# Two feeds for TensorE in a windowed-attention and gated feed-forward kernel, and the attention output taken off PSUM by ACT

## The chip, the cores and the metric

One core of one Trainium2 chip runs the kernel. The metric is the device time of one execution in microseconds. Three runs of the kernel before gave 276.29 (median), 275.74 and 276.56.

## The reference

The input is x of 2048 rows and 448 columns. The output is x plus an attention branch plus a gated feed-forward branch, both on the same normalised rows:

```python
H = 16; Dh = D // H; W = 256                      # D = 448, Dh = 28
qkv = (x @ wqkv) ...                              # q, k, v per head
scores = einsum("bhqd,bhkd->bhqk", q, k) * (Dh ** -0.5)
mask = (idx[:, None] - idx[None, :] >= 0) & (idx[:, None] - idx[None, :] < W)
p = softmax(where(mask, scores, -1e9))
A = einsum("bhqk,bhkd->bhqd", p, v) ... @ wo
B = (gelu(xn @ w_gate) * (xn @ w_up)) @ w_down    # F = 1792
out = x + A(xn) + B(xn)                           # xn = layernorm(x)
```

Each row attends to itself and the 255 rows ahead of it.

## The kernel before

The rows are worked in four blocks (`qb`) of 512 queries. A block has an attention stage and a gated stage, and the work of its neighbours is filled in between.

The attention stage (`attention`) runs over four head groups `g` of four heads each, and for each over three portions `n` of key tiles. A portion computes scores `sc` on TensorE (L373; two PSUM tiles of two banks each, tag "s"), two Exps on ACT into `p_sb` (L378), and the mask on Pool by affine selects (L384). Two portions later `finish` multiplies by the values into `ov` (L348; one bank, tag "o"). The values carry a column of ones, so `ov` also has the softmax's sums. After the third portion of a head group VectorE takes `ov` out: a transpose (L353), a copy of the sums to `l_all` (L354), a reciprocal (L356), a transpose back (L358) and a multiplication by `ov` into `oN` (L359). Both L353 and L359 read `ov` in PSUM. The last two portions of a block are finished by `rest`, which the gated stage calls ahead of its step f=2.

Between the portions `feed` issues other TensorE work, a share at a time. It holds a list of generators and takes the first one to its end before it goes to the next. For blocks 1 and 2 the list is `gen_down(qb - 1)`, the output projection of the block before (for each row tile four matmuls by `wo`, L247, and fourteen by `wd`, L251, into one bank `po`, then VectorE adds x, L256, and SP writes the rows out), and then `gen_proj(qb + 1)`: transposes `tp` of the next block's rows (L177, copied to `xnT`, L178), values `pv` (L205 casts them to `v_sb`), queries and keys `pq`, `pk` (L221, L222 cast them to `qT`, `kT`). In block 3 the second generator is `gen_up`, which makes the `up` half `ue` of the last gated stage ahead of time. All of these take their banks from tag "m", three banks. `aux` brings statistics (L144) and normalisation (L158) of the next block's rows to VectorE, one step after each portion, two calls a portion.

The gated stage (`gated`) runs over the 14 column tiles of F in steps of two: gate `gt` (tag "s") and up `u` (three of four from "m", the fourth from "o"), gelu on ACT (L318), and the product `hT` on VectorE (L320). In each step of two the last 64 rows of the depth are taken by "halves" (L187), two of which run side by side. ACT loads the tables of exp and gelu by turns (L451, L458).

The order of each engine's instructions is that in which the program issues them; tiles of one tag wait until the last reader of the bank is done. Ahead of block 0 stand the loads on SP's and ACT's queues (L89 to L114), warming matmuls `wps`, normalisation of block 0, its values, the padded copies `wqp`, `wkp`, `w3p` of the query and key weights, and the queries and keys of head group 0.

Of the kernel before, what the change touches and what calls it, by code (L numbers as in the profile page):

```python
# [24 lines left out]
class Feed:  # L25


    def __init__(self):
        self.gens = []
        self.left = 0  # L30

    def add(self, gen, ns):
        self.gens.append(gen)
        self.left += ns

    def run(self, ns):
        while ns > 0 and self.gens:
            try:
                c = next(self.gens[0])
                ns -= c  # L40
                self.left -= c
            except StopIteration:
                self.gens.pop(0)

    def share(self, parts):

        self.run(max(self.left, 0) / parts if parts > 1 else 1e12)


@with_exitstack  # L50
def kernel(
# [26 lines left out]
    wraw = blk.tile([P, 4, 2 * D], bf16, name="wraw", tag="hT", bufs=1)  # L78
# [57 lines left out]
    def warmup(n):  # L136
        for _ in range(n):
            wps = psum.tile([P, QB], f32, name="wps", tag="m", bufs=3)
# [15 lines left out]
    def norm(t):  # L154
        xn = work.tile([P, 4, P], bf16, name="xn", bufs=4)
        xf = xn[:, :, :].rearrange("p a b -> p (a b)")
        for lo, n, src in ((0, D, 0), (D, 64, 384)):
            nc.vector.tensor_scalar(out=xf[:, lo:lo + n], in0=x_sb[:, t, src:src + n], scalar1=mv_all[:, t, 0:1],  # L158
# [3 lines left out]
    def gen_prep(qb):  # L162

        for t in range(4 * qb, 4 * qb + 4):
            stat(t)
            yield
        rstd(4 * qb, 4)
        yield
        for t in range(4 * qb, 4 * qb + 4):
            norm(t)  # L170
            yield

    def transp(t, copy):
        xn = xns.pop(t)
        tp = psum.tile([P, 4, P], bf16, name="tp", tag="m", bufs=3)
# [14 lines left out]
    done = set()  # L190

    def gen_v(qb, ts):

        for t in ts:
            pvs = []
            for i in range(2):
                pv = psum.tile([P, QB], f32, name="pv", tag="m", bufs=3)
# [6 lines left out]
            for i in range(2):  # L204
                (nc.vector.tensor_copy if qb else nc.scalar.copy)(out=v_sb[:, t + i, :, 0:Dh], in_=pvs[i][:, 0:D].rearrange("p (h d) -> p h d", d=Dh))  # L205
            yield 390

    def gen_qk(qb, gs):

        ts = slice(qb * QB, (qb + 1) * QB)  # L210
        for g in gs:
            hs = slice(4 * g, 4 * g + 4)
            pq = psum.tile([P, QB], f32, name="pq", tag="m", bufs=3)
            mm3(pq[:, :], lambda c: wqp[:, c, hs, :].rearrange("p h d -> p (h d)"), lambda c: xnT[:, c, ts], True, False)
            yield 650
            pk = psum.tile([P, QB], f32, name="pk", tag="m", bufs=3)
# [7 lines left out]
            yield 1050  # L224
# [14 lines left out]
    def gen_down(qb):  # L239

        hT, oN = hTs[qb], oNs[qb]
        for tt in range(4):
            t = 4 * qb + tt
            cs = slice(tt * P, (tt + 1) * P)
            po = psum.tile([P, QB], f32, name="po", tag="m", bufs=3)
# [12 lines left out]
            yield 375  # L258

    def new_hT(qb):  # L260
        hT = blk.tile([P, NF, QB], bf16, name="hT", tag="hT", bufs=1)
        hTs[qb] = hT
# [10 lines left out]
    def gen_up(qb, fs):  # L273

        ts = slice(qb * QB, (qb + 1) * QB)
        for f in fs:
            us = [psum.tile([P, QB], f32, name="ue", tag="m", bufs=3) for _ in range(2)]
# [7 lines left out]
            yield 1050  # L285

    def gated(qb, early, then):
# [4 lines left out]
        for f in range(0, NF, 2):  # L292
            if f == 2:
                then()
# [11 lines left out]
            for _ in range(2):  # L306
                tag, n = ("m", 3) if nu % 4 < 3 else ("o", 1)
                us.append(psum.tile([P, QB], f32, name="u0", tag=tag, bufs=n))
                nu += 1
            three(gt[:, 0, :], f, True, ts, True, False)  # L310
            three(us[0][:, :], f, False, ts, True, False)
            half(gt[:, 0, :], f, True, 0, ts, False, True)
            half(us[0][:, :], f, False, 1, ts, False, True)
            half(gt[:, 1, :], f + 1, True, 0, ts, True, False)
            half(us[1][:, :], f + 1, False, 1, ts, True, False)
            three(gt[:, 1, :], f + 1, True, ts, False, True)
            three(us[1][:, :], f + 1, False, ts, False, True)
# [17 lines left out]
    def attention(qb, feed, aux, lag):  # L335
        oN = blk.tile([P, 4, QB], bf16, name="oN")
        oNs[qb] = oN
        pend = []
        o_t = {}

        def finish(g, n, pc, p_sb):
# [9 lines left out]
            if n == 2:  # L351
                l1 = work.tile([P, 16, 32], f32, name="l1", bufs=2)
                nc.vector.transpose(out=l1[:, :, :].rearrange("p a b -> p (a b)"), in_=ov[:, :])  # L353
                nc.vector.tensor_copy(out=l_all[:, 4 * qb + g, :], in_=l1[:, :, Dh])  # L354
# [241 lines left out]
```

## Time and profile before

| | us | share of the span |
|---|---|---|
| profiled execution | 276.25 | |
| its span, first to last instruction | 274.5 | |
| TensorE busy | 239.5 | 87% |
| VectorE busy | 150.1 | 55% |
| ACT busy | 133.7 | 49% |
| Pool busy | 75.7 | 28% |

Mean granted TensorE clock: 0.975. Busy times are those of the one profiled execution. A time in square brackets behind a row is how long the engine stood idle ahead of it, and what ended that. Matmuls overlap, so the starts of consecutive groups tell more than the durations of single ones. Start times count from the span's start.

### The profile page before, as it was taken

The numbers are of one execution on the slowest core, as the hardware profiler recorded it, in microseconds if no ns is written. First come the engines' busy times: TensorE is split into PE (matmuls) and PEld (weight loads), VectorE is DVE, ScalarE is ACT, GpSimd is POOL, SyncE is SP. The second block draws the span as 40 slices with busy tenths as digits, with TensorE's granted clock in tenths as the row PEclk, the third lists the DMA queues.
The fourth block names the chain that finished last, engine by engine and source line by source line (L and its number), as shares of the span: only waits on it lengthen the run. The fifth ranks groups of instructions, "written<-read, shape, count | busy, mean of one in ns | idle before, by whom it ended". The sixth has DMA issues, their size and how long they took to land.

```text
span 274.5 us, 4234 instructions
## 1 busy us (share of the span) xinstructions
PE 239.5 (87%) x1695; PEld 93.3 (34%) x1714; DVE 150.1 (55%) x294; ACT 133.7 (49%) x154; POOL 75.7 (28%) x104
## 2 busy tenths in 40 slices
PE   7867877889999969779999988797999998899992
PEld 2323322233344523223334442232334442233450
DVE  6579687423363865653363875744342167856410
ACT  4554456313386646613366583652337656765200
POOL 6222545000034553400006443510004444530000
PEclk9999999979999989999999997999999999999997
DMA  7999500000001100000000010000000010000010
GB/s 201 362 260 268 190 2 0 0 0 4 0 1 35 33 4 0 0 2 0 0 0 19 18 36 0 2 0 0 2 0 17 19 35 2 0 0 2 17 35 26
DMA packets 9025, 10.94 MB, mean 40 GB/s; under 512 B 616, under 2 KB 7976, under 8 KB 9000
## 3 DMA queue, kind: packets, MB, share of 16 engines
q1 hardware_dynamic: 8552, 10.27, 12.7%
q10 hardware_dynamic: 448, 0.34, 0.5%
q8 instruction: 15, 0.25, 0.4%
q14 instruction: 10, 0.08, 0.1%
HBM read 8.77 MB, written 1.84 MB: 39 GB/s over the span
## 4 chain that ended last, share of the span: by engine, by line
PE 67%; DVE 19%; ACT 6%; issue 2%; DMA 2%; POOL 1%; SPq 0%; ACTq 0%; DVEq 0%; POOLq 0%
PE po L251 14%; PE gt L182 14%; PE u L182 8%; PE ov L348 4%; PE gt L187 4%; PE sc L373 4%; PE po L247 4%; PE pv L182 3%; ACT p_sb L378 3%; DVE rb L358 3%; DVE oN L359 3%; DVE l L353 3%; PE ue L182 3%; PE pq L182 2%; ACT ge L318 2%
## 5 line engine op out<-in xcount | busy, mean ns | idle before, releaser
L378 ACT ACTIVATE p_sb<-sc 128x1024 bf16<-128x1024 f32 (+2 forms) x96 | 87.7, 968 | 56.3 <-PE sc L373 53.1
L384 POOL TENSOR_SCALAR_AFFINE_SELECT p_sb<-p_sb 128x512 bf16<-128x512 bf16 (+1 forms) x92 | 69.5, 778 | 162.8 <-ACT p_sb L378 162.8
L320 DVE TENSOR_TENSOR hT<-ge,u 128x512 bf16<-128x512 bf16 x42 | 27.0, 684 | 47.1 <-ACT ge L318 47.1
L318 ACT ACTIVATE ge<-gt 128x1024 bf16<-128x1024 f32 x21 | 21.5, 1024 | 53.7 <-PE gt L182 53.7
L251 PE MATMUL po<-wd,hT 128*128 128x448 bf16 x224 | 47.3, 353 | 0.0
L182 PE MATMUL gt<-xnT,wg 128*128 128x512 bf16 x164 | 45.8, 389 | 1.0 <-ACT p_sb L378 0.8
L182 PE MATMUL u<-xnT,wu 128*128 128x512 bf16 x123 | 34.6, 385 | 0.2
L251 PEld LDWEIGHTS <-hT 128*128 128x128 bf16 x224 | 20.6, 98 | 20.7 <-issue 3.2
L373 PE MATMUL sc<-qT,kT 32*128 32x128 bf16 (+2 forms) x352 | 22.2, 281 | 4.2 <-ACT p_sb L378 1.7
L348 PE MATMUL ov<-p_sb,v_sb 128*32 128x128 bf16 (+2 forms) x352 | 18.3, 286 | 8.6 <-DVE oN L359 8.2
L182 PEld LDWEIGHTS <-wu 128*128 128x128 bf16 x168 | 15.6, 99 | 20.3 <-issue 4.2
L182 PEld LDWEIGHTS <-wg 128*128 128x128 bf16 x168 | 13.8, 99 | 24.2 <-issue 12.8
L256 DVE TENSOR_TENSOR res<-po,x_sb 128x448 bf16<-128x448 f32 x16 | 9.9, 620 | 18.6 <-PE po L251 18.6
L187 PE MATMUL u<-xnT,wgu 64*128 64x512 bf16 x42 | 13.2, 382 | 5.9 <-DVE oN L359 5.9
L221 DVE CAST qT<-pq 128x512 bf16<-128x512 f32 x16 | 11.0, 686 | 13.4 <-PE pk L187 13.4
L158 DVE TENSOR_SCALAR xn<-x_sb,mv_all,rstd_all 128x448 bf16<-128x448 bf16 (+1 forms) x32 | 12.6, 441 | 8.7 <-ACT rstd_all L150 8.6
L182 PE MATMUL pv<-wv,xnT 128*128 128x448 bf16 x48 | 12.0, 379 | 4.8 <-DVE v_sb L205 4.4
L353 DVE STREAM_TRANSPOSE l<-ov 128x512 f32<-128x512 f32 x16 | 11.4, 710 | 8.1 <-PE ov L348 8.1
L187 PE MATMUL gt<-xnT,wgu 64*128 64x512 bf16 x49 | 15.3, 382 | 0.0
L247 PE MATMUL po<-wo,oN 128*128 128x448 bf16 x64 | 14.8, 353 | 0.0
L182 PE MATMUL pk<-xnT,wkp 128*128 128x512 bf16 x46 | 12.9, 379 | 2.0 <-DVE qT L221 1.9
L348 PEld LDWEIGHTS <-v_sb 128*32 128x32 bf16 x352 | 6.0, 95 | 23.5 <-issue 19.5
(66 smaller groups left out, 214.6 us busy)
## 6 DMA issues: line engine op xcount, KB each, us to landing
out_dram<-res SPq DMA_DIRECT2D x16, 112.0 KB, 1.7
wd<-in_B_w_down_dram SPq DMA_DIRECT2D x1, 1568.0 KB, 13.3
wu<-in_B_w_up_dram SPq DMA_DIRECT2D x1, 1344.0 KB
wg<-in_B_w_gate_dram SPq DMA_DIRECT2D x1, 1344.0 KB, 16.6
x_sb<-in_A_x_dram SPq DMA_DIRECT2D x1, 896.0 KB
wraw<-in_A_wqkv_dram SPq DMA_DIRECT2D x1, 672.0 KB, 7.9
x_sb<-in_A_x_dram SPq DMA_DIRECT2D x1, 448.0 KB
wo<-in_A_wo_dram SPq DMA_DIRECT2D x4, 98.0 KB
```

The lines of the kernel that those rows point to most:

```text
L158: nc.vector.tensor_scalar(out=xf[:, lo:lo + n], in0=x_sb[:, t, src:src + n], scalar1=mv_all[:, t, 0:1], scalar2=rstd_all[:, t:t + 1], op0= ...
L182: nc.tensor.matmul(ps, lhsT=lhs(c), rhs=rhs(c), start=start and c == 0, stop=stop and c == 2, skip_group_check=True)
L187: nc.tensor.matmul(ps, lhsT=lhs[p0:p0 + 64], rhs=rhs[p0:p0 + 64], start=start, stop=stop, tile_position=(p0, 0), skip_group_check=True)
L247: nc.tensor.matmul(po[:, 0:D], lhsT=oN[:, g, cs], rhs=wo[:, g, :], start=(g == 0), stop=False, skip_group_check=True)
L251: nc.tensor.matmul(po[:, 0:D], lhsT=hT[:, f, cs], rhs=wd[:, f, :], start=False, stop=(f == NF - 1), skip_group_check=True)
L318: nc.scalar.activation(out=ge[:, :, :], in_=gt[:, :, :], func=ACT.Gelu_apprx_tanh)
L320: nc.vector.tensor_tensor(out=hT[:, f + i, :], in0=ge[:, i, :], in1=us[i][:, :], op=ALU.mult)
L348: nc.tensor.matmul(ov[32 * j:32 * j + 32, q0:q0 + nq], lhsT=v_sb[:, kt, h, :], rhs=p_sb[:, j, col:col + nq], start=(n == 0 and i == 0), st ...
L353: nc.vector.transpose(out=l1[:, :, :].rearrange("p a b -> p (a b)"), in_=ov[:, :])
L373: nc.tensor.matmul(ss[j // 2][:, j % 2, col:col + nq], lhsT=kT[r, g, kt * P:(kt + 1) * P], rhs=qT[r, g, qb * QB + q0:qb * QB + q0 + nq], s ...
L378: nc.scalar.activation(out=p_sb[:, 2 * i:2 * i + 2, 0:ncol], in_=ss[i][:, :, 0:ncol], func=ACT.Exp, scale=SCALE)
L384: nc.gpsimd.affine_select(out=reg, in_=reg, pattern=mid + [[1 if diag else -1, P]], compare_op=ALU.is_ge, fill=0.0, base=0 if diag else -1 ...
```

## The change

- The output projection and the next block's projections become two feeds. `share` hands out both in portions. A generator marks the end of a closed group (one whose banks are now being evacuated) by a negative number, and `share` then takes the other feed, if that one has work left for this portion.
- PSUM: "m" has two banks, and a bank "d" is new. `gen_down` takes "o" for its first tile, then "d". Values, queries and keys of block 0 and of block 1's projections go round "m", "m", "d" (`bank`), later ones use "m". In the gated stage `u` takes by turns two "m", or "d" and "o". `hT` has two buffers.
- The attention output is copied out of `ov` by ACT (`oc`). VectorE's transposes read `oc` and are issued behind the portion's fed work (`inverse`). The multiplication into `oN` is done by Pool, behind the affine selects of the portion after (`scale_o`).
- Statistics of blocks 2 and 3 are made in the gated stages of blocks 0 and 1; `rstd` and `norm` of the next block stand ahead of the attention (`prep`). Those of block 1 are made early in block 0.
- At the start two loads change queues, two `xnT` copies go from ACT to VectorE, and the first queries and keys come ahead of the second pair of values. The gated stage's first step issues `u` ahead of `gt`.

```diff
+    def run(self, ns):
+        ran = 0
+        while ran < ns and self.gens:
             try:
                 c = next(self.gens[0])
+                self.closed = c < 0
+                c = abs(c)
+                ran += c
                 self.left -= c
...
+def share(feeds, parts):
+    want = [max(f.left, 0) / parts if parts > 1 else 1e12 for f in feeds]
+    last = None
+    while any(f.gens and w > 0 for f, w in zip(feeds, want)):
+        can = [i for i, f in enumerate(feeds) if f.gens]
+        if last in can and len(can) > 1 and feeds[last].closed and want[1 - last] > -800:
+            can.remove(last)
+        last = max(can, key=lambda i: min(want[i], feeds[i].left))
+        want[last] -= feeds[last].run(1)
...
     for p0 in (0, 64):
-        nc.scalar.dma_start(out=wv[p0:p0 + 64, 3, :], in_=A_wqkv[384:448, 2 * D:3 * D])
-    nc.sync.dma_start(out=wraw[:, 0:3, :], in_=rows(A_wqkv, 0, 3)[:, :, 0:2 * D])
+        nc.sync.dma_start(out=wv[p0:p0 + 64, 3, :], in_=A_wqkv[384:448, 2 * D:3 * D])
+    nc.scalar.dma_start(out=wraw[:, 0:3, :], in_=rows(A_wqkv, 0, 3)[:, :, 0:2 * D])
...
+    ring = [("m", "m", "d"), 0]
+    def bank(name):
+        tag = ring[0][ring[1] % len(ring[0])]
+        ring[1] += 1
+        return psum.tile([P, QB], f32, name=name, tag=tag, bufs=2 if tag == "m" else 1)
...
-    def gen_down(qb):
+    def gen_down(qb, tags="dddd"):
...
-            po = psum.tile([P, QB], f32, name="po", tag="m", bufs=3)
+            po = psum.tile([P, QB], f32, name="po", tag=tags[tt], bufs=2 if tags[tt] == "m" else 1)
...
-            for _ in range(2):
-                tag, n = ("m", 3) if nu % 4 < 3 else ("o", 1)
+            for tag, n in ((("m", 2), ("m", 2)), (("d", 1), ("o", 1)))[nu % 2]:
                 us.append(psum.tile([P, QB], f32, name="u0", tag=tag, bufs=n))
...
+        def inverse():
+            while copied:
+                g, oc = copied.pop(0)
+                l1 = work.tile([P, 16, 32], f32, name="l1", bufs=1)
+                nc.vector.transpose(out=l1[:, :, :].rearrange("p a b -> p (a b)"), in_=oc[:, :])
+                nc.vector.tensor_copy(out=l_all[:, 4 * qb + g, :], in_=l1[:, :, Dh])
+                ri = work.tile([P, 16], f32, name="ri")
+                nc.vector.reciprocal(out=ri[:, :], in_=l_all[:, 4 * qb + g, :])
+                rb = work.tile([P, 16, 32], f32, name="rb", bufs=2)
+                nc.vector.transpose(out=rb[:, :, :], in_=ri[:, :].unsqueeze(2).to_broadcast([P, 16, 32]))
+                later.append((g, oc, rb))
+
+        def scale_o():
+            while later:
+                g, oc, rb = later.pop(0)
+                nc.gpsimd.tensor_tensor(out=oN[:, g, :], in0=oc[:, :], in1=rb[:, :, :].rearrange("p a b -> p (a b)"), op=ALU.mult)
...
             if n == 2:
...
-                nc.vector.tensor_tensor(out=oN[:, g, :], in0=ov[:, :], in1=rb[:, :, :].rearrange("p a b -> p (a b)"), op=ALU.mult)
+                oc = work.tile([P, QB], f32, name="oc", bufs=2)
+                nc.scalar.copy(out=oc[:, :], in_=ov[:, :])
+                copied.append((g, oc))
...
-                for _ in range(2):
-                    next(aux, None)
-                feed.share(12 - 3 * g - n)
+                scale_o()
+                left = 12 - 3 * g - n
+                if qb and left > 10:
+                    feeds[0].share(left / 2)
+                else:
+                    share(feeds, left + 0.4 if left > 1 else 1)
+                inverse()
+                next(aux, None)
...
-    transp(2, nc.scalar.copy)
-    norm(3)
-    transp(3, nc.scalar.copy)
-    warmup(3)
+    norm(3, nc.vector)
+    transp(2, nc.vector.tensor_copy)
+    transp(3, nc.vector.tensor_copy)
+    warmup(2)
...
-    for _ in gen_v(0, (2,)):
-        pass
+    stat(4)
+    for gen in (gen_qk(0, (0,)), gen_v(0, (2,))):
+        for _ in gen:
+            pass
+    stat(5)
...
-            feed.add(gen_down(qb - 1), DOWN)
+            ring[0] = ("m",)
+            feeds = [Feed(gen_down(qb - 1, "oddd"), DOWN)]
             if qb < 3:
-                feed.add(gen_proj(qb + 1), PROJ)
-                aux = gen_prep(qb + 1)
+                feeds.append(Feed(gen_proj(qb + 1), PROJ))
+                prep(qb + 1)
...
+        hooks = {2: rest}
+        if qb < 2:
+            for i in range(4):
+                hooks[4 + 2 * i] = lambda t=4 * qb + 8 + i: stat(t)
```

## Rows read from the trace of the kernel before

**Rows 1.** Busy time by stretch: length, PE, PEld, DVE, ACT, POOL, clock, DMA.

```profile
142.03:179.40 37.37, 33.29 (x299) 13.70 (x300) 23.82 (x50) 23.28 (x26) 17.25 (x22) 0.95 0.04 14
...
206.89:242.50 35.61, 33.04 (x289) 12.60 (x292) 18.56 (x33) 22.90 (x24) 17.25 (x22) 1.00 0.04 14
```

**Rows 2.** Who waited for whom, TensorE: us in total, times, longest us.

```profile
PE ov L348 <- DVE oN L359: 8.2, 6, 1.8
PE u L187 <- DVE oN L359: 5.9, 3, 2.1
PE pv L182 <- DVE v_sb L205: 4.4, 2, 2.2
```

**Rows 3.** The chain of waits from 162 to 167 us: start, us, what.

```profile
162.30 0.73 DVE l L353
163.05 0.43 DVE l_all L354
...
164.54 0.69 DVE oN L359
...
165.81 1.28 PE pv L182 x3
```

**Rows 4.** Busy time by stretch, the columns of rows 1: four shorter stretches.

```profile
165.81:168.61 2.80, 2.79 (x22) 0.63 (x21) 1.48 (x3) 0.00 (x0) 0.69 (x1) 0.50 0.00 0
...
190.71:193.94 3.23, 3.23 (x18) 1.20 (x17) 1.27 (x2) 1.02 (x1) 0.00 (x0) 1.00 0.00 0
16.09:28.00 11.91, 9.44 (x84) 3.82 (x86) 11.13 (x27) 7.43 (x11) 4.04 (x6) 1.00 1.06 254
28.00:47.89 19.89, 14.77 (x125) 5.38 (x125) 14.89 (x27) 10.45 (x16) 9.43 (x14) 1.00 0.17 57
```

**Rows 5.** Instructions in order of time, TensorE, block 2: start, us, instruction, idle before.

```profile
140.76 0.39 PE L373 MATMUL sc<-qT,kT 32*128 32x128 bf16 x6 [0.35 <-ACT ge L318]
...
144.01 0.39 PE L373 MATMUL sc<-qT,kT 32*128 32x384 bf16 x6 [0.21 <-ACT p_sb L378]
...
176.98 0.40 PE L348 MATMUL ov<-p_sb,v_sb 128*32 128x128 bf16 x8 [1.58 <-DVE oN L359]
...
179.37 0.82 PE L182 MATMUL gt<-xnT,wg 128*128 128x512 bf16 x3
...
187.16 0.39 PE L187 MATMUL u<-xnT,wgu 64*128 64x512 bf16 x1 [1.90 <-DVE oN L359]
...
205.04 0.23 PE L373 MATMUL sc<-qT,kT 32*128 32x128 bf16 x2
```

**Rows 6.** Instructions in order of time, TensorE, start and block 0.

```profile
7.85 1.31 PE L182 MATMUL pv<-wv,xnT 128*128 128x448 bf16 x6 [0.43 <-DMA wv<-in_A_wqkv_dram]
...
30.54 0.40 PE L348 MATMUL ov<-p_sb,v_sb 128*32 128x128 bf16 x8 [1.25 <-DVE oN L359]
...
47.89 0.81 PE L182 MATMUL gt<-xnT,wg 128*128 128x512 bf16 x3 [0.76 <-ACT p_sb L378]
...
75.31 0.23 PE L373 MATMUL sc<-qT,kT 32*128 32x128 bf16 x2
```

**Rows 7.** Groups by line and shape, ACT and Pool: busy us, mean ns, idle.

```profile
L378 ACT ACTIVATE p_sb<-sc 128x512 bf16<-128x512 f32 x8 | 4.3, 594 | 8.2 <-PE sc L373 8.2
...
L149 ACT ACTIVATE lnv<-mv_all,eps_t 128x4 f32<-128x4 f32 x3 | 0.9, 298 | 0.5 <-DVE mv_all L145 0.5
...
L384 POOL TENSOR_SCALAR_AFFINE_SELECT p_sb<-p_sb 128x1024 bf16<-128x1024 bf16 x28 | 30.8, 1101 | 115.2 <-ACT p_sb L378 115.2
```

**Rows 8.** Instructions in order of time, VectorE, block 0, and one of block 2.

```profile
14.74 0.69 DVE L221 CAST qT<-pq 128x512 bf16<-128x512 f32 x1 [2.75 <-PE pk L187]
...
27.15 0.70 DVE L353 STREAM_TRANSPOSE l<-ov 128x512 f32<-128x512 f32 x1
...
30.31 0.41 DVE L178 COPY xnT<-tp 128x512 bf16<-128x512 bf16 x1
...
185.17 0.17 DVE L354 COPY l_all<-l 128x16 f32<-128x16 f32 x1
```

More of the change, by code (lines that the diff above doesn't have):

```diff
@@ L25, with __init__ @@
 class Feed:
[L28 to L34, printed above, removed]
+    def __init__(self, gen=None, ns=0):
+        self.gens = [gen] if gen else []
+        self.left = ns
+        self.closed = False
     def run(self, ns):
-        while ns > 0 and self.gens:
+        ran = 0
+        while ran < ns and self.gens:
             try:
                 c = next(self.gens[0])
-                ns -= c
+                self.closed = c < 0
+                c = abs(c)
+                ran += c
                 self.left -= c
@@ L196, in gen_v @@
             for i in range(2):
-                pv = psum.tile([P, QB], f32, name="pv", tag="m", bufs=3)
+                pv = bank("pv")
                 cs = slice((t + i) * P, (t + i + 1) * P)
@@ L204, in gen_v @@
             for i in range(2):
-                (nc.vector.tensor_copy if qb else nc.scalar.copy)(out=v_sb[:, t + i, :, 0:Dh], in_=pvs[i][:, 0:D].rearrange("p (h d) -> p h d", d=Dh))
-            yield 390
+                (nc.vector.tensor_copy if qb or (t and i) else nc.scalar.copy)(out=v_sb[:, t + i, :, 0:Dh], in_=pvs[i][:, 0:D].rearrange("p (h d) -> p h d", d=Dh))
+            yield -390
     def gen_qk(qb, gs):
@@ L276, in gen_up @@
         for f in fs:
-            us = [psum.tile([P, QB], f32, name="ue", tag="m", bufs=3) for _ in range(2)]
+            us = [psum.tile([P, QB], f32, name="ue", tag="m") for _ in range(2)]
             three(us[0][:, :], f, False, ts, True, False)
@@ L284, in gen_up, with gated @@
             nc.vector.tensor_copy(out=hTs[qb][:, f + 1, :], in_=us[1][:, :])
-            yield 1050
-    def gated(qb, early, then):
+            yield -1050
+    def gated(qb, early, hooks):
         ts = slice(qb * QB, (qb + 1) * QB)
@@ L333, in pieces, with attention @@
         return [(k - 1, 0, 256, 0), (k + 2, 256, 256, 256)], [(128, 1, False), (256, 1, True)]
-    def attention(qb, feed, aux, lag):
+    def attention(qb, feeds, aux, lag):
         oN = blk.tile([P, 4, QB], bf16, name="oN")
         oNs[qb] = oN
-        pend = []
+        pend, copied, later = [], [], []
         o_t = {}
+        def inverse():
[13 more added lines that the diff above has]
+                nc.gpsimd.tensor_tensor(out=oN[:, g, :], in0=oc[:, :], in1=rb[:, :, :].rearrange("p a b -> p (a b)"), op=ALU.mult)
         def finish(g, n, pc, p_sb):
@@ L351, in finish @@
             if n == 2:
-                l1 = work.tile([P, 16, 32], f32, name="l1", bufs=2)
-                nc.vector.transpose(out=l1[:, :, :].rearrange("p a b -> p (a b)"), in_=ov[:, :])
-                nc.vector.tensor_copy(out=l_all[:, 4 * qb + g, :], in_=l1[:, :, Dh])
-                ri = work.tile([P, 16], f32, name="ri")
-                nc.vector.reciprocal(out=ri[:, :], in_=l_all[:, 4 * qb + g, :])
-                rb = work.tile([P, 16, 32], f32, name="rb", bufs=2)
-                nc.vector.transpose(out=rb[:, :, :], in_=ri[:, :].unsqueeze(2).to_broadcast([P, 16, 32]))
-                nc.vector.tensor_tensor(out=oN[:, g, :], in0=ov[:, :], in1=rb[:, :, :].rearrange("p a b -> p (a b)"), op=ALU.mult)
+                oc = work.tile([P, QB], f32, name="oc", bufs=2)
+                nc.scalar.copy(out=oc[:, :], in_=ov[:, :])
+                copied.append((g, oc))
+        if qb:
+            feeds[0].run(1)
         for g in range(4):
             while (qb, g) not in done:
-                feed.run(1)
+                feeds[0].run(1)
             for n in range(3):
@@ L405 @@
     rstd(2, 1)
-    norm(1)
+    norm(1, nc.vector)
     warmup(2)
```

94 lines of the change are left out of this document (48 added, 46 removed).

## Prediction, made before the changed kernel was run

> **What bounds the kernel now.** I read the stages first: the busy time of each engine in stretches. From the second block on the kernel repeats: an attention stage, then a gated stage. TensorE is busy 33.29 of 37.37 us in the attention stage of block 2 and 33.04 of 35.61 us in that of block 3 [rows 1]. No other engine comes near that, so TensorE bounds these stages, and what can be won is its idle time and the time in which it runs slowly. Next I read whom TensorE waits for. It is VectorE nearly every time: `ov` and `u` wait for `oN` (8.2 and 5.9 us in all) and `pv` for `v_sb` (4.4 us) [rows 2]. Third, the chain of waits shows how one of them arises: two transposes with small steps between them start at 162.30, the multiplication `oN` at 164.54, and only then comes the cast of `v_sb` that frees a PSUM bank; `pv` goes on at 165.81 [rows 3]. The output projection, which could have filled that hole, has run earlier: one feed serves all of it first and then the projections. Fourth, the clock: behind that wait the granted clock is 0.50 for 2.80 us, while a gated step has 1.00 [rows 4]. 0.50 is the lower of the two levels, 1.2 instead of 2.4 GHz, and 2.80 us of matmuls at it lose 1.40 us.
>
> In block 0 it is different: from 16.09 to 28.00 VectorE is busy 11.13 of 11.91 us and TensorE 9.44, so there VectorE sets the pace; from 28.00 to 47.89 TensorE is busy only 14.77 of 19.89 us [rows 4].
>
> **The change part by part.** The profiled execution took 276.25 us, 274.5 us of span and 1.75 us around it; the median of the runs is 276.29, so the sum holds for both.
>
> *Waits on the attention output.* Bank "o" is held today until the multiplication has read it. Afterwards ACT copies it out and it is free after one copy. An ACT instruction of 128x512 from PSUM takes 0.594 us [rows 7]; the next writer of "o" comes a whole portion later (two to three us). The copy waits for `ov`; behind it on ACT stand the next two Exps, whose scores follow `ov` on TensorE anyway, so they lose at most the copy. ACT is busy 23.28 of 37.37 us [rows 1] and bears 4 x 0.6 more. In the gated stage the second `u` of step f=2 uses "o", and its wait of 1.90 us [rows 5] goes too: the copy then ends ahead of the moment at which this bank is wanted. VectorE loses 16 x 0.69 us, but its transposes keep their place in the order only in part: they are now issued behind the evacuations of the same portion.
>
> *The multiplication on Pool.* Nothing of before shows a multiplication there. The nearest row is the affine select over 1024 elements, 1.1 us [rows 7]. From below I take half of it, 0.55 us, for 512 elements; from above twice it, 2.2, if f32 costs double. I take 1.1 us, since two operands of 512 are 1024 elements read. Behind the waiting multiplication on Pool stand the affine selects of the next portion, for which `ov` waits two portions later. Pool is busy 17.25 of 37.37 us [rows 1], so I cost it at nothing; the cover is gone only past 3.8 us (rival C). The Trainium skill, "GPSIMD Engine Reference", "Elementwise — side-by-side cycle accounting", speaks against this move: a two-input operation takes Pool about 2.6 cycles an element at 1.2 GHz, some twice VectorE's time. By that it would be an estimated 1.1 us; the sum would be the same, and C is the less likely for it. No run so far shows it.
>
> *Two feeds.* `po` gets bank "d", the projections keep two banks "m", and `share` changes feeds after each closed group. I wrote the order out by its rules. In blocks 1 and 2 behind each closed group of the projections stands `ov`/`sc` or 0.4 to 1.1 us of output projection, before the freed bank is wanted: the wait of `pv` goes, and with it the slow stretch behind it. One place stays tight: `pq` of group 0 comes when VectorE still works on the transposes of head group 0, some 0.3 us. The first portions run only the output projection, in "o" and then "d".
>
> *Start of a block.* `prep` now stands ahead of the attention: two small ACT operations, of 0.3 [rows 7] and 0.2 us, are put between the table load and the first Exp, and the scores of portion 2 need both Exps. They waited 0.21 us for ACT [rows 5]; with 0.5 us more and the output projection started earlier that becomes 0.9, so 0.7 lost. The wait of 0.35 us for the last gelu [rows 5] goes, since four matmuls of `po` now stand ahead of the scores. The statistics go to gated steps, where VectorE has room: a step takes 3.23 us and VectorE works 1.27 of it [rows 4].
>
> So for the attention stage of block 2 (and 1, the same): won are 2.2 (`pv`), 1.58 (`ov` [rows 5]), 1.4 (clock), 0.35; lost 0.7 and 0.3: net 4.5. For its gated stage, 179.37 to 205.04 [rows 5]: the 1.90 us and the restart behind it, 2.1. Two blocks: 13.2.
>
> *Block 0.* Today VectorE casts `qT` from 14.74 and copies the last `xnT` at 30.31, till 30.72, with `l` to `oN` of head group 0 in between, from 27.15 to 30.31 [rows 8]. Afterwards the first query projection stands ahead of the second value pair (some 1.5 us of matmuls: six take 1.31 [rows 6], and their halves), but two `xnT` copies of 0.41 move to VectorE ahead of the weights and cost back 0.8: the first cast at about 14.0. The stream (15.98 us today, 14.74 to 30.72) then loses the 3.16 us chain, which comes behind it, and gains one cast of 0.7: 14.0 + 15.98 - 3.16 + 0.7 = 27.5. Then one transpose and the first value pair, 1.8: `ov` of head group 1 comes at 29.3 instead of 30.54 [rows 6]. From there the work is the same; of the 5.12 us of idle TensorE from 28.00 to 47.89 [rows 4] 3.87 lie behind 30.54, nearly all behind `oN` or banks that wait in the same line. I take 3.7 of it as won: gated stage at 42.9 instead of 47.89 [rows 6], 5.0 won. The gated stage of block 0 is 27.42 us long [rows 6], 1.75 longer than that of block 2, by the slow clock behind the same wait for `oN`: 2.1 + 1.8 = 3.9 won.
>
> *Loads.* The halves of `wv` move to SP's queue, behind `wv`, and `wraw` to ACT's. The first `pv` already waits 0.43 us for `wv` [rows 6]; sharing with `wraw` can cost up to 1.5 us (a quarter of the six that `wv` takes from its issue to 7.85) or win those 0.4. `wraw` itself is now wanted about 1.2 us later and has that slack. I take 0 and keep both ends.
>
> *Block 3* has no `prep`. 2.57 us idle in its attention stage [rows 1], of which I count 1.9 won: a little stays at the second portion, and two banks for `ue` are enough because output matmuls stand between. Its gated stage and the last output stage don't stand among the waits of any size [rows 2] and stay.
>
> Sum: 5.0 + 3.9 + 13.2 + 1.9 = 24.0; 276.25 - 24.0 = 252.3 us (rounded).
>
> **The rivals.**
>
> A: *waits move to the smaller banks.* With two banks "m" and one "d" each evacuation that stands behind the transposes stops TensorE. The chain without its multiplication is still 2.24 us long, 162.30 to 164.54 [rows 3]; behind it an evacuation of 0.7 (a cast in [rows 8]); TensorE has some 1.7 us of other work meanwhile: 1.2 us at each of 12 head groups whose chain lies in an attention stage, 15 us at all of them, 8 us at about half: 260. For it: the chain and the single bank "d". Against it: the order that I wrote out puts matmuls of the other feed behind nearly every closed group. Some VectorE instructions get longer while Pool works: the small copy `l_all` took 0.43 us at 163.05 [rows 3] and 0.17 at 185.17, when Pool was idle [rows 8]. The Trainium skill, "SBUF — State Buffer", "SBUF: two separate sides", says that Pool and certain VectorE instructions lock one port pair and the loser waits for the whole instruction of the other; the trace agrees, and by that rule each of the 16 new Pool multiplications could hold a VectorE copy for its length, which would raise A by up to an estimated 1 us per head group. From the rows alone A gets 0.14.
>
> B: *the order does not come out.* If the feeds run down at unlike speed, so that the projections again stand alone at the end, `pv` and the slow clock stay, and only `ov` and `u` are won: 8.2 + 5.9 + 1.8 = 15.9, so 260 to 261. The written-out order speaks against it: 0.05.
>
> C, on the other side: *Pool becomes the bound.* Per head group Pool has 17.25 + 1.2 over four, 4.6 us, of affine selects, and TensorE some 8.4. A multiplication of over 3.8 us makes Pool the longer one; from 1.5 us beyond (24.0 over 16 head groups), about 5.3 us, the kernel is slower than before; at 6 us it is 276 + 11 = 287. My upper bound is 2.2 us. For it only that nothing of before shows the operation: 0.04.
>
> D: *more comes back.* The waits at a block's start and for `pq` don't arise, `wv` lands earlier, and the restarts behind each wait go too: 1.0 x 2 + 0.4 + 0.5 a stage, some 6 us more: 246. 0.09.
>
> **How the numbers follow.** The sum has 0.68, with 248 to 256 as its own range (1.5 us for the loads, 1 us a block for small waits). A 0.14, B 0.05, C 0.04, D 0.09. The range from 246 to 261 leaves out the far half of A, C and the low half of D, under 0.2. About 0.3% (0.8 us) is what a measurement tells from no change. All cases but C are faster: 0.95; an end within 0.3% only by several of them together, 0.01; slower 0.04.
>
> **What would show it.** Right: no `ov` or `u` behind `oN` any more, no `pv` behind `v_sb` above 0.5 us, the granted clock at 1.00 through the attention stages, periods of blocks 1 and 2 of 58 instead of 64.9 us, the first gated stage near 42.9. Wrong: `po`, `pq` or `ue` behind a cast or `res` at many places (A); projections alone in the last portions (B); the affine selects behind the Pool multiplication and `ov` behind those (C). It would also be wrong if TensorE's clock fell in block 0, where short waits follow one another, or if `wv` landed late.

## The result, and the profile after

The changed kernel takes 253.03 us (median of 4 runs, 252.17 to 253.59), against 276.43 us (275.74 to 277.57) of the kernel before beside it: a ratio of 0.915 with an interval of 0.911 to 0.919. Forecast were 252.3 us and a range from 246 to 261. The profiled execution took 252.17 us, of which 250.4 us are span.

First the page of the kernel after: busy time of each engine, then the chain of work that ended last, followed back from the last instruction, by engine.

```profile
PE 233.8 (93%) x1690; PEld 91.9 (37%) x1713; DVE 137.9 (55%) x281; ACT 140.0 (56%) x167; POOL 95.9 (38%) x120
...
PE 82%; DVE 7%; ACT 3%; DMA 3%; issue 1%; POOL 1%; SPq 0%; ACTq 0%; POOLq 0%
```

And that chain in the kernel before:

```profile
PE 67%; DVE 19%; ACT 6%; issue 2%; DMA 2%; POOL 1%; SPq 0%; ACTq 0%; DVEq 0%; POOLq 0%
```

TensorE fills 82% of the chain, where it was 67% before; VectorE fell there from 19% to 7%. So what is left is almost TensorE's own work. Next, whom TensorE waited for in the kernel after, to be read beside [rows 2] (total us, times, longest us):

```profile
PE sc L409 <- ACT p_sb L414: 1.7, 4, 0.6
...
PE tp L186 <- DVE qT L238: 1.4, 1, 1.4
PE pv L191 <- DMA wv<-in_A_wqkv_dram: 0.8, 1, 0.8
PE gt L191 <- ACT p_sb L414: 0.7, 1, 0.7
...
PE ov L387 <- POOL p_sb L420: 0.2, 1, 0.2
```

No `ov` and no `u` stands behind `oN` any more, no `pv` behind `v_sb`. The largest sum left is `sc` waiting for an Exp: 0.46 us at the start of blocks 1 and 2, and 0.19 and 0.58 us in the last head group of block 0, which are in the kernel before as well. The stretches of the kernel after, in the columns of [rows 1]: attention stage of block 1, its gated stage, attention stage of block 3, and 3.7 us in block 0.

```profile
67.36:101.12 33.76, 33.05 (x310) 13.69 (x312) 18.15 (x37) 25.29 (x30) 18.70 (x24) 1.00 0.04 11
101.12:124.41 23.29, 22.93 (x126) 8.64 (x128) 14.96 (x30) 10.04 (x11) 4.76 (x5) 1.00 0.02 6
181.47:217.39 35.92, 34.53 (x301) 13.15 (x305) 17.24 (x29) 25.77 (x29) 19.67 (x24) 1.00 0.04 11
...
26.70:30.40 3.70, 3.70 (x32) 1.59 (x28) 2.39 (x6) 2.07 (x4) 1.49 (x3) 0.66 1.00 321
```

In the attention stage TensorE is busy 33.05 of 33.76 us, at a granted clock of 1.00. The place that [rows 3] showed looks like this after; first TensorE in block 1, then VectorE at the same place of block 2:

```profile
79.01 1.30 PE L191 MATMUL pv<-wv,xnT 128*128 128x448 bf16 x6
80.24 0.40 PE L387 MATMUL ov<-p_sb,v_sb 128*32 128x256 bf16 x8
80.58 0.40 PE L409 MATMUL sc<-qT,kT 32*128 32x384 bf16 x8
80.91 0.36 PE L196 MATMUL pv<-wv,xnT 64*128 64x448 bf16 x2
81.20 0.93 PE L268 MATMUL po<-wd,hT 128*128 128x448 bf16 x4
81.98 1.29 PE L191 MATMUL pv<-wv,xnT 128*128 128x448 bf16 x6
```

```profile
138.36 1.16 DVE L222 CAST v_sb<-pv 128x448 bf16<-128x448 f32 x2 [2.42 <-PE pv L196]
139.43 0.70 DVE L367 STREAM_TRANSPOSE l<-oc 128x512 f32<-128x512 f32 x1
...
140.74 0.71 DVE L372 STREAM_TRANSPOSE rb<-ri 128x512 f32<-128x512 f32 x1
141.37 1.12 DVE L222 CAST v_sb<-pv 128x448 bf16<-128x448 f32 x2
```

Between two value pairs (`pv` x6) now stands one step of the output projection (`po`), and no matmul waits. On VectorE the two casts that free the banks of `pv` come first, and the transposes stand behind them; in [rows 3] it was the other way round.

Where the 24.1 us of span went (274.5 to 250.4), from one stage's first matmul to the next: the attention stage of block 0 begins at 15.76 instead of 16.09 and its gated stage at 44.22 instead of 47.89; block 1 begins at 67.36 instead of 75.31, so 7.95 are won by then. Blocks 1 and 2 take 57.05 instead of 64.87 us each: 15.6. The attention stage of block 3 takes 35.92 instead of 37.42: 1.5. The last gated stage, with the output projection behind it, gives back 0.1, and behind the last store's issue 0.9 more passes till the end. 7.95 + 15.6 + 1.5 - 0.1 - 0.9 = 24.1.

### The profile page after: what moved, and what is told of

It is laid out like the page before. It is cut to its first block, busy times and chain, and to the rows that moved or that the text cites. A ratio compares the mean times of both kernels' runs of the same rounds, so it can differ in the third digit from the quotient of the medians.

```text
span 250.4 us, 4258 instructions
## 1 busy us (share of the span) xinstructions
PE 233.8 (93%) x1690; PEld 91.9 (37%) x1713; DVE 137.9 (55%) x281; ACT 140.0 (56%) x167; POOL 95.9 (38%) x120
## 4 chain that ended last, share of the span: by engine, by line
PE 82%; DVE 7%; ACT 3%; DMA 3%; issue 1%; POOL 1%; SPq 0%; ACTq 0%; POOLq 0%
PE po L268 16%; PE gt L191 16%; PE u L191 10%; PE sc L409 6%; PE ov L387 5%; PE gt L196 5%; PE po L264 4%; PE pv L191 4%; PE ue L191 4%; PE pq L191 3%; PE pk L191 3%; DMA wv<-in_A_wqkv_dram 3%; ACT p_sb L414 2%; PE pq L196 2%; PE tp L186 1%
## 5 line engine op out<-in xcount | busy, mean ns | idle before, releaser
L268 PE MATMUL po<-wd,hT 128*128 128x448 bf16 x224 | 49.8, 354 | 0.0
L191 PE MATMUL gt<-xnT,wg 128*128 128x512 bf16 x162 | 43.3, 381 | 1.2 <-ACT p_sb L414 0.7
L191 PE MATMUL u<-xnT,wu 128*128 128x512 bf16 x123 | 33.1, 379 | 0.2
L268 PEld LDWEIGHTS <-hT 128*128 128x128 bf16 x224 | 19.9, 98 | 20.7 <-issue 4.6
L378 POOL TENSOR_TENSOR oN<-oc,rb 128x512 bf16<-128x512 f32 x16 | 20.6, 1288 | 15.4 <-DVE rb L372 15.4
L409 PE MATMUL sc<-qT,kT 32*128 32x128 bf16 (+2 forms) x352 | 21.2, 277 | 1.9 <-ACT p_sb L414 1.7
L191 PE MATMUL pq<-xnT,wqp 128*128 128x512 bf16 x41 | 12.5, 381 | 0.5 <-issue 0.2
L196 PE MATMUL u<-xnT,wgu 64*128 64x512 bf16 x42 | 12.6, 381 | 0.0
L392 ACT COPY oc<-ov 128x512 f32<-128x512 f32 x16 | 9.4, 585 | 5.7 <-PE ov L387 5.7
```

What stands on the lines that cost most here:

```text
L191: nc.tensor.matmul(ps, lhsT=lhs(c), rhs=rhs(c), start=start and c == 0, stop=stop and c == 2, skip_group_check=True)
L196: nc.tensor.matmul(ps, lhsT=lhs[p0:p0 + 64], rhs=rhs[p0:p0 + 64], start=start, stop=stop, tile_position=(p0, 0), skip_group_check=True)
L268: nc.tensor.matmul(po[:, 0:D], lhsT=hT[:, f, cs], rhs=wd[:, f, :], start=False, stop=(f == NF - 1), skip_group_check=True)
L378: nc.gpsimd.tensor_tensor(out=oN[:, g, :], in0=oc[:, :], in1=rb[:, :, :].rearrange("p a b -> p (a b)"), op=ALU.mult)
L409: nc.tensor.matmul(ss[j // 2][:, j % 2, col:col + nq], lhsT=kT[r, g, kt * P:(kt + 1) * P], rhs=qT[r, g, qb * QB + q0:qb * QB + q0 + nq], s ...
```

## Experiments

Each kernel is the kernel after with one edit (two in the run called "both"), except the first, which is the kernel before with one part of the change. The edits are shown in part; "..." stands where lines are left out. "Period" is the time from the first scores of one block to those of the next; of block 1 it is 64.87 us before and 57.06 after.

**The attention output alone.** The kernel before, with its one feed, its loads and its order of VectorE's work; only the copy by ACT and the multiplication on Pool are added.

```
+                oc = work.tile([P, QB], f32, name="oc", bufs=2)
+                nc.scalar.copy(out=oc[:, :], in_=ov[:, :])
-                nc.vector.transpose(out=l1[:, :, :].rearrange("p a b -> p (a b)"), in_=ov[:, :])
+                nc.vector.transpose(out=l1[:, :, :].rearrange("p a b -> p (a b)"), in_=oc[:, :])
...
-                nc.vector.tensor_tensor(out=oN[:, g, :], in0=ov[:, :], in1=rb[:, :, :].rearrange("p a b -> p (a b)"), op=ALU.mult)
+                later.append((g, oc, rb))
...
+        def scale_o():
+            while later:
+                g, oc, rb = later.pop(0)
+                nc.gpsimd.tensor_tensor(out=oN[:, g, :], in0=oc[:, :], in1=rb[:, :, :].rearrange("p a b -> p (a b)"), op=ALU.mult)
...
+                scale_o()
...
+            scale_o()
```

> The kernel before with the attention output alone changed: ACT copies ov out, VectorE's transposes read the copy, Pool multiplies; one feed, three banks m, no bank d. Theory (two separate causes, as in the prediction's sum): the waits of ov and u for oN go (8.2 + 5.9 us and 1.8 us of slow clock in block 0), the wait of pv for v_sb and the slow clock behind it stay: 276.3 - 15.9 = 260 us, 259 to 262. Rival (the order of the feeds is the only cause): over 270 us. Rival (freeing bank o early is all): under 255 us.

Measured: 260.43 us (260.34 to 260.88), ratio 0.940 (0.932 to 0.947), period 61.21. Whom TensorE waited for:

```profile
PE pv L182 <- DVE v_sb L205: 4.2, 2, 2.1
PE pk L182 <- DVE qT L221: 2.2, 3, 1.6
```

All waits on `oN` are gone, the two of `pv` stay as in [rows 2]. The copy and the multiplication moved alone bring 16 us, as rival B's sum had it (15.9). The place fits too: the period of block 0 is 52.57 instead of 59.22 us, those of blocks 1 and 2 are 61.2 instead of 64.87. The edit both frees bank "o" early and takes 16 x 0.69 us from VectorE; the run with the multiplication on VectorE, below, bears on which of the two counts.

**Everything but that.** The kernel after, but VectorE takes `ov` out of PSUM at once, with transposes and multiplication, as before.

```
-                oc = work.tile([P, QB], f32, name="oc", bufs=2)
-                nc.scalar.copy(out=oc[:, :], in_=ov[:, :])
-                copied.append((g, oc))
+                nc.vector.transpose(out=l1[:, :, :].rearrange("p a b -> p (a b)"), in_=ov[:, :])
...
+                nc.vector.tensor_tensor(out=oN[:, g, :], in0=ov[:, :], in1=rb[:, :, :].rearrange("p a b -> p (a b)"), op=ALU.mult)
...
-                inverse()
```

> The changed kernel with the attention output as before: VectorE transposes ov out of PSUM and multiplies, at the place of the last ov. Two feeds, banks m, d, start and statistics as changed. Theory (two causes): ov and u wait for oN again, up to 14 us and the clock behind u, so 262 to 269 us. Rival (the order of the feeds is the only cause): 252 to 255 us.

Measured: 285.6 us (284.84 to 287.06), ratio 1.029 (1.021 to 1.037): slower than before. Its first scores come at 20.04 instead of 16.09, which is 4 us of it, but its periods are long too: 67.5 and 65.8. TensorE's waits, and VectorE in block 1:

```profile
PE u L196 <- DVE oN L381: 7.9, 3, 2.7
PE ov L370 <- DVE oN L381: 4.6, 5, 1.8
PE pv L191 <- DVE v_sb L222: 4.4, 2, 2.2
PE po L264 <- DVE res L273: 4.0, 3, 2.1
```

```profile
92.36 0.72 DVE L375 STREAM_TRANSPOSE l<-ov 128x512 f32<-128x512 f32 x1 [1.81 <-PE ov L370]
...
94.70 0.69 DVE L381 TENSOR_TENSOR oN<-ov,rb 128x512 bf16<-128x512 f32 x1
95.31 1.14 DVE L222 CAST v_sb<-pv 128x448 bf16<-128x448 f32 x2
```

The expectation took the two gains as independent and was wrong. With `ov` taken out by VectorE, the casts still stand behind the whole chain, and the projections now have two banks and the output projection one: `pv` waits as before (4.4), and `po` joins it (4.0). This is the mechanism of rival A, and here it costs more than the second feed brings.

**Is it the second feed?** The kernel after, with one feed: the whole output projection first, then the projections, in the same banks.

```
-                feeds.append(Feed(gen_proj(qb + 1), PROJ))
+                feeds[0].gens.append(gen_proj(qb + 1))
+                feeds[0].left += PROJ
...
-                feeds.append(Feed(gen_up(3, early), UP1 * len(early)))
+                feeds[0].gens.append(gen_up(3, early))
+                feeds[0].left += UP1 * len(early)
```

Taken out as well is the rule by which the first portions of a block run the output projection alone; with one feed it has no meaning.

> The changed kernel with one feed in blocks 1 to 3: all of the output projection first, then the projections (in block 3 the ue matmuls). Theory: the holes at the casts of v_sb come back in blocks 1 and 2 (2.2 us and 1.4 us of slow clock each) and at two banks m more of them: 259 to 265 us. Rival (bank release is all, the order does nothing): 252 to 254 us.

Measured: 264.81 us (262.65 to 267.57), ratio 0.952 (0.943 to 0.961), periods 62.8. The profiled execution, 267.57 us, is the longest of the four by its start (first scores at 20.90); its periods stand at a granted clock of 1.00. Two of TensorE's waits:

```profile
PE po L264 <- DVE res L273: 3.6, 5, 0.7
PE u L191 <- DVE qT L238: 2.7, 2, 1.3
```

The time is above rival B's 260 to 261, and the periods are longer than that of the first experiment (61.2). Both waits are for PSUM banks: `po` now has one, and `u` takes two that the projections use, where before three served them all. So the smaller banks without the mixing are the likely loss; the two kernels differ in more than the banks, so this is argued. The mixing itself, with all else as after, is worth 5.7 us a block.

**Is it the change of feed after a closed group?** The kernel after, where the feed that lags goes on, whether or not it has just closed a group.

```
-        if last in can and len(can) > 1 and feeds[last].closed and want[1 - last] > -800:
-            can.remove(last)
```

> The changed kernel without the rule that share leaves a feed behind a closed group; it takes the feed that is owed most. Theory: the switch is what covers the evacuations, so without it pq, pk or po wait 0.3 to 0.7 us for a cast at up to ten places in each of blocks 1 to 3: 255 to 265 us. Rival (mixing the two feeds by their shares covers them without the rule): 252 to 254 us.

Measured: 253.89 us (252.95 to 254.44), ratio 0.915 (0.907 to 0.922), periods 58.0. The rule is worth 0.95 us a block, by periods that repeat within 0.01 us; the totals overlap with those of the kernel after. My own expectation made too much of it. That the two feeds run side by side at the right speed does nearly all.

**Is it the order on VectorE?** The kernel after, but the chain of transposes goes back to its place ahead of the portion's casts. ACT still copies and Pool still multiplies, but Pool's multiplication, which is issued behind the chain, also comes one portion earlier.

```
                 copied.append((g, oc))
+                inverse()
...
-                inverse()
                 next(aux, None)
```

> The changed kernel with VectorE's chain (two transposes, copy, reciprocal) issued at the last ov of a head group, ahead of the portion's casts, instead of behind the portion's fed work; ACT's copy and Pool's multiplication as changed. Theory (what made two feeds alone slow is that the chain stands ahead of the casts, with two banks m): pv or pq wait 1 to 2 us for a cast at most head groups, the period of blocks 1 and 2 goes from 57.05 to 59 to 62 us, 257 to 263 us in all. Rival (it was bank o held by VectorE's multiplication): period below 58, 252 to 254 us.

Measured: 263.97 us (263.39 to 266.44), ratio 0.958 (0.949 to 0.967), periods 60.19. TensorE's waits, VectorE and the late matmul:

```profile
PE pv L191 <- DVE v_sb L222: 3.5, 2, 1.8
PE po L264 <- DVE res L273: 3.5, 3, 1.8
```

```profile
85.15 0.71 DVE L367 STREAM_TRANSPOSE l<-oc 128x512 f32<-128x512 f32 x1 [2.43 <-ACT oc L392]
...
86.47 0.71 DVE L372 STREAM_TRANSPOSE rb<-ri 128x512 f32<-128x512 f32 x1
87.10 1.12 DVE L222 CAST v_sb<-pv 128x448 bf16<-128x448 f32 x2
```

```profile
87.74 1.30 PE L191 MATMUL pv<-wv,xnT 128*128 128x448 bf16 x6 [1.77 <-DVE v_sb L222]
```

The time went 1 us over what was expected; the place is as expected. The casts come 2 us later, `pv` waits 1.77 us although a `po` step stands ahead of it (85.04, four matmuls). `ov` waits only 0.4 us for Pool in all, so Pool's earlier place is not the cause. So this move, four instructions (2.0 us) moved behind the casts, is worth 11 us beside the two feeds (12 against the kernel after in the same series, below): a third piece. Without it the feeds do not pay: the attention output alone stood at 260.43.

**Pool's multiplication on VectorE.** At the same place of the order.

```
-                nc.gpsimd.tensor_tensor(out=oN[:, g, :], in0=oc[:, :], in1=rb[:, :, :].rearrange("p a b -> p (a b)"), op=ALU.mult)
+                nc.vector.tensor_tensor(out=oN[:, g, :], in0=oc[:, :], in1=rb[:, :, :].rearrange("p a b -> p (a b)"), op=ALU.mult)
```

> The changed kernel with the multiplication oc by rb on VectorE instead of Pool, at the same place of the program. Theory (neither engine bounds the stage): VectorE has 18 of 33.8 us in the attention stage of block 1, so 11 us more over the kernel are hidden: 252 to 254 us. Rival (Pool's 16 multiplications hold VectorE's copies): 1 to 3 us faster, 249.5 to 252. Rival (VectorE's order matters, the multiplication stands ahead of a cast): 255 or more.

Measured: 258.27 us (255.02 to 258.57), ratio 0.927 (0.916 to 0.938). The period is 58.16, 1.1 us more than after, from one wait a block of `pq` for `v_sb` (1.0 us):

```profile
PE pq L191 <- DVE v_sb L222: 2.0, 2, 1.0
```

The multiplication at 88.26 (below) stands ahead of that cast, so the last rival is right about the order, at 1.1 us a block. So VectorE's lighter load is worth little beside the early release of bank "o"; this is argued from the changed kernel, since the first experiment moved both. Most of the rest of the 5 us by which the time is over the forecast of 252 to 254 lies ahead of the first of these multiplications: the first scores of the profiled execution come at 19.60 instead of 15.76. Two of its VectorE instructions, and Pool at the same time (x2 is two affine selects, the second of 1.10 us, to 88.85):

```profile
88.26 1.13 DVE L378 TENSOR_TENSOR oN<-oc,rb 128x512 bf16<-128x512 f32 x1
...
99.37 0.69 DVE L378 TENSOR_TENSOR oN<-oc,rb 128x512 bf16<-128x512 f32 x1
```

```profile
87.16 1.69 POOL L420 TENSOR_SCALAR_AFFINE_SELECT p_sb<-p_sb 128x512 bf16<-128x512 bf16 x2 [1.31 <-ACT p_sb L414]
...
99.86 1.29 POOL L420 TENSOR_SCALAR_AFFINE_SELECT p_sb<-p_sb 128x512 bf16<-128x512 bf16 x2 [1.84 <-ACT p_sb L414]
```

**Pool's multiplication three and five times** (the loop below with 3 or 5 around the instruction), to find where Pool's cover ends.

```
+                for _ in range(3):
+                    nc.gpsimd.tensor_tensor(out=oN[:, g, :], in0=oc[:, :], in1=rb[:, :, :].rearrange("p a b -> p (a b)"), op=ALU.mult)
```

> The changed kernel with the Pool multiplication done three times over (the same result each time): 3 x 1.29 = 3.87 us a head group. Theory of the prediction: the cover is gone past 3.8 us, so this stands at its edge: 252 to 256 us. Rival (Pool was already near the path): three times 1.29 adds 2.6 us at each of 12 to 16 head groups, 280 or more.

Measured, three times: 263.9 us (263.13 to 266.92), ratio 0.955 (0.943 to 0.966), period 59.57. Expected was nearly nothing, since 3.96 us fill Pool's free time about exactly. Pool and TensorE in the attention stage of block 1:

```profile
99.93 3.96 POOL L379 TENSOR_TENSOR oN<-oc,rb 128x512 bf16<-128x512 f32 x3
103.84 2.29 POOL L421 TENSOR_SCALAR_AFFINE_SELECT p_sb<-p_sb 128x1024 bf16<-128x1024 bf16 x3
```

```profile
105.00 0.24 PE L388 MATMUL ov<-p_sb,v_sb 128*32 128x128 bf16 x4 [0.92 <-POOL p_sb L421]
```

```profile
PE ov L388 <- POOL p_sb L421: 8.1, 15, 1.5
```

`ov` waits 15 times for the affine selects, 8.1 us in all. Pool is not full on average (24.00 of 35.42 us from block 1's first scores to its gated stage); the multiplication stands in its queue ahead of selects that `ov` wants soon.

> The changed kernel with the Pool multiplication done five times over: 6.4 us a head group. Theory: Pool has 4.6 + 6.4 = 11.0 us a head group against 8.4 of TensorE, 2.6 us over at 12 head groups (the last of a block runs on in the gated stage): 276 to 290 us, with the affine selects standing behind the multiplications and ov behind the affine selects. Rival (affine selects have more slack than counted): under 265.

Measured, five times (6.65 us a head group), in one run: 293.2 us, where 276 to 290 was expected, periods 64.93, `ov` behind the selects 23.3 us in all. First scores at 20.76, so 5 us of the time belong to the start. Without these it would stand at some 288, 12 us above before: rival C's mechanism is real. A straight line from 263.9 us at 3.96 to 288 at 6.65 reaches the time of before at an estimated 5.3 us, where the prediction had put it; but the cost begins well ahead of its 3.8.

**The start.** Loads in their old queues (halves of `wv` on ACT's, `wraw` on SP's); the key casts of block 0's last three groups on ACT; both; and the kernel after once more beside them.

```
-        nc.sync.dma_start(out=wv[p0:p0 + 64, 3, :], in_=A_wqkv[384:448, 2 * D:3 * D])
+        nc.scalar.dma_start(out=wv[p0:p0 + 64, 3, :], in_=A_wqkv[384:448, 2 * D:3 * D])
-    nc.scalar.dma_start(out=wraw[:, 0:3, :], in_=rows(A_wqkv, 0, 3)[:, :, 0:2 * D])
+    nc.sync.dma_start(out=wraw[:, 0:3, :], in_=rows(A_wqkv, 0, 3)[:, :, 0:2 * D])
...
-            nc.vector.tensor_copy(out=kT[:, g, ts], in_=pk[:, :])
+            (nc.vector.tensor_copy if qb or g == 0 else nc.scalar.copy)(out=kT[:, g, ts], in_=pk[:, :])
```

> The changed kernel with the two loads back on their queues: the halves of wv on ACT's queue, wraw on SP's behind wv. In the eight profiles of kernels with the changed loads the first pv began at 7.75 to 10.53 us, in those with the old ones at 7.26 and 7.85. Theory (the changed loads make wv late by 0.6 to 3 us, and TensorE's clock falls while it waits): first pv at 7.2 to 7.9 us, first scores at 15.0 to 15.5, median 1 to 2.5 us below the changed kernel in the same call. Rival (the spread is that of the chip's loads, whatever the queue): no difference, both spread over 3 us.

> The changed kernel with the casts of the keys of head groups 1 to 3 of block 0 on ACT instead of VectorE (3 x 0.68 us off VectorE). Theory (VectorE sets the pace of block 0 until the transposes): the waits of tp (1.38 and 0.55 us) and most of the slow clock behind them go, block 0's gated stage starts 2 to 3 us earlier: 250 to 251 us. Rival (ACT's copies hold the Exps, and scores and ov wait for those): 252.5 to 254.

> Both: the loads on their old queues and the casts of keys of block 0's head groups 1 to 3 on ACT. Theory (the two add): 2.2 us for the casts (first scores to the next block's scores 50.25 instead of 52.45 us in the run with the casts alone) and 1 to 2.5 us for the loads: 248 to 250 us, the fastest of all. Rival: wv is not what sets the start, 250 to 252.

> The changed kernel once more, beside the two others on the same chip: 252 to 254 us. All theories say the same; it is what the others are compared with.

Measured: after again 252.08 us (251.48 to 253.0), ratio 0.913 (0.909 to 0.917); old loads 251.42 (249.8 to 251.65), 0.908 (0.903 to 0.913); key casts on ACT, with the new loads and on another chip, 251.54 (248.65 to 253.58), 0.909 (0.898 to 0.919), where two of the four runs, 248.65 and 250.26, have a mean granted clock of 0.99 and two, 252.83 and 253.58, one of 0.98; both 249.05 (248.95 to 249.57), 0.902 (0.898 to 0.906). The old loads alone are 0.7 us, with overlapping intervals, so less than expected; in their profile the scores come at 15.37, 1.27 us ahead of those in the profile beside it (16.64), but the period of block 0 is 52.37 instead of 51.17 and the clock is down there. Both together are 3.0 us below the kernel after beside them: the lowest median measured. The two better runs of the key casts alone lie at 249.5 on average, on their chip, so most of the gain can be theirs. With the casts on ACT block 0 has a period of 50.25 us in both profiles. With them on VectorE and nothing in block 0 changed, it has 51.17 in three profiles (after again, one feed, no switch) and 52.45 and 52.37 in two in which the clock fell in block 0 (after, old loads). So VectorE still set the pace of block 0, by 0.9 us at a full clock. That the clock then no longer falls there holds for two profiles, which is too few to show it.

## Why the prediction was right, point by point

**The waits on `oN`.** Right, in mechanism and size: none is left, and alone they bring 16.0 us, where 15.9 were added up. ACT bears the copies (16 of 585 ns); what `sc` and `gt` still wait for Exps, 2.4 us in all, is at the starts of two blocks, at the end of block 0's attention stage (0.77 us, as before) and at one gated stage.

**Pool.** The multiplication takes 1.288 us, where 1.1 was taken; it hides. The Trainium skill's rate in "GPSIMD Engine Reference", "Elementwise — side-by-side cycle accounting", gave an estimated 1.11; the trace is 16% above that. The stated end of the cover, 3.8 us, was wrong: it was worked out as a mean over a head group, and 3.96 us already cost 11. What ends it is the place in Pool's queue, ahead of selects for `ov`. Since the true price is a third of it, nothing hung on this. The prediction also thought it possible that each multiplication would hold a VectorE copy for up to 1 us: `l_all` took 0.17 or 0.18 us in 14 of 16 cases, and 0.55 and 0.57 in the two that began beside an affine select, not beside a multiplication.

**Two feeds.** The forecast was right that `pv` and the slow clock behind it go. Its reason was incomplete. It put the effect down to the change of feed after each closed group; that rule is worth 0.95 us a block. And it gave half a sentence and no price to the transposes being issued behind the portion's evacuations; that is worth 11 us. Rival A had assumed the chain still ahead of the casts; where this was put back, A's waits came, at 264 us, and without ACT's copy at 285.6. What kept A from coming true is an order on VectorE which the prediction had named and not used; to that extent it was luck that A had only 0.14.

**Sizes.** Blocks 1 and 2: 7.82 us each came, 6.6 were forecast. The attention stage gave 5.43 (39.19 to 33.76) instead of 4.5: the 0.3 for `pq` did not arise, and the scores at a block's start wait 0.46 us (71.71) instead of 0.9, since ACT's table load, two small operations and first Exp (125.06 to 126.79 in block 2) run beside the output projection that begins at 124.41. The last 0.2 us are open. (The prediction's 37.37 us for this stage begin at 142.03, 1.85 us behind its first scores at 140.18; from those it is 39.19. No term of the sum hangs on it.) The gated stage gave 2.38 instead of 2.1. Block 3: 1.5 of 1.9. Its gated stage was said to stay; it waits 0.71 us for an Exp, as block 0's did before [rows 6].

**Block 0.** The gated stage begins at 44.22 instead of the forecast 42.9. In the second profile of the same kernel, it is 43.83 after a start 0.88 us later, so 27.19 us of attention stage (by the forecast 42.9 - 16.09 = 26.8, if the first scores stay where they were). The difference of the two profiles is the clock, which the prediction had named as what could spoil it. The page's row of granted clock, in 40 slices of 6.3 us, of the first profile and then of the second, and the same 3.7 us in each (clock 0.66 in the stretches above, so part of it at the lower level, 1.2 GHz; 1.00 here, all at 2.4):

```profile
PEclk9999799999999999999999999999999999999997
```

```profile
PEclk9999999999999999999999999999999999999998
```

```profile
26.70:30.40 3.70, 3.65 (x39) 1.69 (x39) 3.05 (x8) 2.55 (x5) 2.00 (x4) 1.00 1.02 312
```

Both profiles have the same two waits ahead of it, of a transpose for `qT` (1.38 us) and for `xnT` (0.55 us). So the waits alone do not decide whether the clock falls; what does was not found. The gated stage itself is 23.14 us long in the first profile, 4.3 less than before, where 3.9 were forecast.

**Loads and end.** Taken as 0 between -0.4 and 1.5. The wait of the first `pv` for `wv` was 0.83 instead of 0.43 us, 1.7 in the second profile, and up to 2.9 in other kernels with the new queues. Between the medians it makes 0.7 us. That the program ends 0.9 us later is most likely no effect of the change: from the end of the last store's issue to the end of the span it is 4.3 us before and 4.6 in the first experiment, but it spreads as much, from 4.6 (key casts on ACT, feeds alone) to 5.2 (after), among kernels with the change.

In sum the misses cancelled, so that the forecast is within 1 us of the time is luck: blocks 1 and 2 gave 2.4 us more than forecast, block 0, block 3, the last gated stage and the end 2.3 less.

## What to carry to other kernels

Before a bank is made smaller, look at what stands on the evacuating engine ahead of the copy that frees it: the same feeds and banks gave 23 us with the casts ahead of VectorE's chain and 12 us with the chain ahead of the casts, and cost 9 us where VectorE's multiplication was put ahead of them too and held bank "o". Two parts of a change that relieve the same engine are not to be added up; one may pay only with the other: the attention output alone gave 16 us, all the rest alone cost 9, together they gave 23. Spare time on an in-order engine is counted from the place in its queue to the next result that someone wants, not as a mean over a stage.

## What the runs showed of the hardware

**VectorE held up by Pool.** The multiplication from PSUM and SBUF took 690 to 693 ns in all 16 cases of the kernel before, five of which began with an affine select under way (at 38.85 beside selects from 37.89 to 39.12). With both operands in SBUF, it takes 691 ns where no Pool instruction is under way at its start, and up to 1469 where one is: at 88.26 it lasts 1.13 us and ends 0.54 us after the select that ran till 88.85; at 99.37, where Pool begins later, it takes 0.69. Seven of the 16 are lengthened, 2.4 us in all. Where the multiplication came first, Pool was held: two selects from 207.62, behind a multiplication at 207.40, took 1.56 us, where two such took 1.23 at 90.03. The Trainium skill, "SBUF — State Buffer", "SBUF: two separate sides", says that a VectorE operation with two SBUF inputs and a Pool operation that reads SBUF lock each other out for a whole instruction, whichever starts first; this agrees. So a copy out of PSUM also exposes the operation behind it to Pool, which leaving it in PSUM did not.

**The same loads land at different times.** With the new queues the first `pv` begins between 7.75 and 10.53 us in ten profiles, with the old between 7.26 and 8.11 in four (the kernel before among them). Where it is late, the clock at the start is sometimes down as well. In eight of the twelve profiles of kernels with the change the first scores come 7.3 us behind that `pv`; in the other four they come 9.5 to 10.7 us behind it, and in all four a slice of the first three has a clock of 7 tenths or less. In the kernel with the multiplication on VectorE `pv` begins at 9.83 and the scores at 19.60; in the second profile of the kernel after, with all slices at 9, at 9.36 and 16.64. Being late does not decide it: without the change of feed `pv` begins at 9.93, and the scores at 17.21. The row of the first:

```profile
PEclk9769889999999999999999999999999999999999
```

That the two queues share what the loads get is argued, not shown; the periods behind the start are not touched by it.
